# Weights in 1 MB transfers with 8192-byte rows, and the values of two attention blocks side by side

## The chip, the cores and the metric

The kernel runs on one core of a Trainium2 chip. The metric is the device time of one execution in microseconds (us): 333.23 us, the median of 3 runs (332.99 to 333.95). Its engines are PE (matrix products), DVE and ACT (element work, both also reading PE's banks), POOL (element work), and SP, which here issues nearly all transfers. All transfers run on the same 16 DMA engines.

## The reference

Three stages, all in float32 outside:

```
attention   B=4, H=8, S=768, D=64; chunks of 32 queries see 16 keys to the left, their own 32,
            8 to the right, and 8 memory keys; softmax; x = out as (3072 tokens, 512)
soft MoE    logits = x @ phi (32 slots); slot_input = softmax over tokens, transposed, @ x
            for each of 8 experts: relu(slot_input[e] @ w1[e]) @ w2[e]   (512x1024, 1024x512)
            x = softmax over slots(logits) @ slot_out
final       h = x @ w_in; solu = h * softmax(h); layer norm times g; @ w_out
```

w1 and w2 are 2 MB for each expert, 32 MB in all; w_in and w_out arrive as 64-bit floats, 4 MB each, and are turned into float32 on the chip.

## The kernel before, in words

**Attention.** The work is 32 blocks (GROUPS), each two heads by half a sequence, 12 chunks. Block g has one array kq (keys and queries, 128 rows of 3200 bytes, 400 KB, `load_qk`, L188) and two halves of values (64 rows of 3120 bytes each, 195 KB, `load_v`, L202), loaded into alternate partitions of one of four zeroed buffers vz. The loop over g issues, in this order: the score products of block g+1 (`emit_qk`, L254), the softmax steps of g+1, the load of kq g+4, weight loads (`load_e`), the value products of block g-1 (`emit_pv`, L310), the load of values g+3 (VLEAD), the transposes of g, and the spreading of kq g+3 into a zero-padded operand by POOL and ACT (`emit_spread`, L303 and L299). SP takes its transfers in that order; a load of kq waits for the products on its old contents, a load of values for `emit_pv(g-1)`.

**Weights.** They are loaded in chunks of 512 KB (128 rows of 4096 bytes) into slots of a list: eight of w_in and seven of w_out alternately, then w1 and w2 by units, then the last of w_out. A unit is half of an expert's w1 or w2, two chunks, 1 MB; there are 32 (`units`), in the order in which PE uses them. LOADS says how many chunks `load_e` issues in each block of the loop (30 in all); after the loop it issues as many as there are free slots. There are 17 slots in the areas e1, e2 and e3, the four of e3 used once only; a slot of w_out (w7); and when the attention's buffers are done, 5 in ex0 (the kq area), 6 in ex1 (the vz area) and one each in ex2 and ex3 (buffers of x). `release` puts a slot back on the list when its chunk has been used: a chunk of w_in when it has been cast, a chunk of a unit behind the products of that unit.

**Units.** After the attention, `emit_w1` (L497) and `emit_w2` (L515) run the 32 units; the transposes between them are L504. Behind each unit its two chunks are released and `load_e` is called. In between stand the casts of w_out and the softmax over slots. Then the final stage runs over 24 tiles of 128 tokens, on PE for the most part (L723).

The program states the order by hand; each engine takes its instructions in that order and waits only for what it needs.

The order of the loads stands in these lines of the loop:

```python
            if g + 4 < GROUPS:
                load_qk(g + 4)
            load_e(LOADS[g])
            if 1 <= g:
                emit_pv(g - 1)
            if g + VLEAD < GROUPS:
                load_v(g + VLEAD)
```

Of the kernel before, what the change touches and what calls it, by code (L numbers as in the profile page):

```python
# [16 lines left out]
P = 128  # L17
# [6 lines left out]
WIN = 64  # L24
REC = CH + NMEM
NREC = NCH + 1
VW = D + 1
NT = B * S
NTILE = NT // P
DM = H * D  # L30
KC = DM // P
E, SE, FF = 8, 4, 1024
NSLOT = E * SE
FC = FF // P
GT = 3
GROUPS = UNITS * 2
# [4 lines left out]
NR = GT * NSLOT  # L41
NE = 25
CAST0, CASTN, NEARLY = 3, 3.4, 8
VLEAD = 3
LOADS = [0] + [1, 1, 1, 0] + [1] * 28
LANE, SIDE = 2.6, 1

CASTU = (0, 1, 2, 3, 4, 5, 6)
# [25 lines left out]
VS = GCH * VW  # L74
# [5 lines left out]
def tile_kernel(ctx: ExitStack, tc: tile.TileContext, kr, vr, w1, w2, w_in, w_out, cst, out):  # L80
    nc = tc.nc
    pe, dve, act, pool, sp = nc.tensor, nc.vector, nc.scalar, nc.gpsimd, nc.sync
# [35 lines left out]
    def at(name, off, n, dt=FP32):  # L118
        o, size, tl = arenas[name]
        assert off + n <= size, (name, off, n, size)  # L120
        v = tl[:, o + off:o + off + n]
        return v if dt == FP32 else v.bitcast(dt)
# [3 lines left out]
    def bank(i):  # L126
        return banks[i]
# [20 lines left out]

    kq = [at("kq", nq * i, nq) for i in range(4)]
    kz = [at("kz", 2 * KS * i, 2 * KS) for i in range(2)]  # L150
    vz = [at("vz", 2 * VS * i, 2 * VS).rearrange("p (h c) -> p h c", h=2) for i in range(4)]
    sb_ = [at("s", GTOK * i, GTOK) for i in range(2)]
    atb = [at("at", GTOK * i, GTOK) for i in range(2)]
    xtb = at("xt", 0, KC * GTOK).rearrange("p (k t) -> p k t", k=KC)
# [4 lines left out]
    w_in_f = at("win", 0, KC * FF)  # L159
    w_in_sb = w_in_f.rearrange("p (k f) -> p k f", k=KC)  # L160
    mhi = at("win", 0, FF, FP32R)
    free = [at(n, 1024 * i, 1024) for n, c in (("e1", 4), ("e2", 9), ("e3", NE - 13 - FC)) for i in range(c)]
    wslot = [at(f"w{j}", 0, 1024) for j in range(FC)]
    once = free[13:]
    free.append(wslot[-1])
    whi, wlo = {}, {}

    sint = at("misc", 0, 128).rearrange("p (k s) -> p k s", k=KC)
# [18 lines left out]
    def load_qk(g):  # L187
        sp.dma_start(out=kq[g % 4], in_=kr[g])  # L188
# [8 lines left out]
            move(on, z[:, :, 0:CH], own)  # L197
            move(on, z[:, :, CH:REC], mem.to_broadcast([64, GREC, NMEM]))

    def load_v(g):  # L200
        for h in range(2):
            sp.dma_start(out=vz[g % 4][h:P:2, h, :], in_=vr[g, h])  # L202

    units = [("w1", 0, 0), ("w1", 0, 1)]
    for e in range(E - 1):
        units += [("w1", e + 1, 0), ("w2", e, 0), ("w1", e + 1, 1), ("w2", e, 1)]
    units += [("w2", E - 1, 0), ("w2", E - 1, 1)]
    chunks = [(w, j) for j in range(2 * KC) for w in ("win", "wout")][:-1]
    for u in units:
        chunks += [u[:2] + (2 * u[2] + j,) for j in range(2)]  # L210
    chunks.append(("wout", FC - 1))
    slot_of = {}
    nxt = [0]

    def more(name, n):

        free.extend(at(name, 1024 * i, 1024) for i in range(n))

    def load_e(n=99):
        while n and nxt[0] < len(chunks):  # L220
            key = chunks[nxt[0]]
            if key[0] == "wout":
                slot = wslot[key[1]]
            elif free:
                slot = free.pop(0)
            else:
                break
            slot_of[key] = slot
            if key[0] in ("w1", "w2"):
                src = (w1 if key[0] == "w1" else w2)[key[1], key[2]]  # L230
                sp.dma_start(out=slot.rearrange("p (k f) -> p k f", k=2), in_=src)
            else:
                src = (w_in if key[0] == "win" else w_out)[key[1]]
                sp.dma_start(out=slot.bitcast(I64), in_=src)
            nxt[0] += 1
            n -= 1

    def release(key):
        if slot_of[key] is wslot[-1]:
            return  # L240
        if key[0] == "win" or not any(slot_of[key] is x for x in once):
            free.append(slot_of[key])


    def kwin(i, c):
# [2 lines left out]
    def emit_qk(g):  # L248
        i = g % 4
        bk = bank(g % 2)  # L250
        for t in range(GT):
            for j in range(4):
                c = t * 4 + j
                pe.matmul(  # L254
                    out=bk[32 * j:32 * j + 32, t * 128:(t + 1) * 128],
                    lhsT=kq[i][:, KT + c * CH:KT + (c + 1) * CH],
                    rhs=kwin(g % 2, c),
                    start=True, stop=True,
                )
# [45 lines left out]
    def emit_pv(g):  # L305
        bk = bank(4 + g % 2)
        for t in range(GT):
            for j in range(4):
                c = t * 4 + j
                pe.matmul(  # L310
                    out=bk[32 * j:32 * j + 32, t * 2 * VW:(t + 1) * 2 * VW],
                    lhsT=atb[g % 2][:, c * CH:(c + 1) * CH],
                    rhs=vz[g % 4][:, :, c * VW:(c + 1) * VW],
                    start=True, stop=True,
                )

# [480 lines left out]

    with tc.manual_schedule():
        for i in range(4):
            for h in range(2):  # L800
                (pool if i < 3 else dve).memset(vz[i][:, h, :], 0.0)
            if i < 2:
                dve.memset(kz[i][0:64, KS:2 * KS], 0.0)
                dve.memset(kz[i][64:128, 0:KS], 0.0)
# [3 lines left out]
        load_qk(2)  # L808
        load_v(0)
        load_qk(3)  # L810
        load_v(1)
        load_v(2)
        emit_spread(0, "ad")
        emit_qk(0)
        emit_spread(1, "ad")
# [18 lines left out]
        for j in range(NEARLY):  # L834
# [4 lines left out]
            out=sel, in_=ident.rearrange("p (t s) -> p t s", t=4)[:, 0:GT, :], axis=AX.X, op=ALU.add  # L839
        )  # L840
        for g in range(GROUPS):
            if g + 1 < GROUPS:
                emit_qk(g + 1)
            if g == GROUPS - 2:
                area("a0", [("ex0", 5 * 1024)])
                more("ex0", 5)
            emit_softmax(g + 1)
            if g + 4 < GROUPS:
                load_qk(g + 4)
            load_e(LOADS[g])  # L850
            if 1 <= g:
                emit_pv(g - 1)
            if g + VLEAD < GROUPS:
                load_v(g + VLEAD)
            for f, hb in todo.get(g, []):
                f(hb)
            emit_t(g)
            if 3 <= g:
                emit_xt(g - 3, copy=False)
            emit_at(g)  # L860
            for f, hb in then.get(g, []):
                f(hb)
            if g + 1 < GROUPS:
                emit_exp(g + 1)
            if 3 <= g:
                emit_xtcopy(g - 3)
            for f, hb in last.get(g, []):
                f(hb)
            if 3 <= g + SPL < GROUPS:
                emit_spread(g + SPL, SPR[g % len(SPR)])  # L870
            for j, i in casts.get(g, []):
                if j not in early:
                    early[j] = win_ops(j, j)
                early[j][i]()
# [40 lines left out]
        for i in range(5, 24, 6):  # L915
            x = cb.pop(i)
# [59 lines left out]
        for x in TAIL[:first]:  # L976
# [12 lines left out]
            e3=e3,  # L989
# [7 lines left out]
def layout(inputs):  # L997
    import numpy as np

    q, k, v = inputs["q"], inputs["k"], inputs["v"]  # L1000
    mk, mv = inputs["mem_k"], inputs["mem_v"]
    f = np.float32
    a = {}
    qv = q.reshape(B, PAIRS, 2, 2, GTOK, D).transpose(0, 3, 1, 2, 5, 4)
    fill = mk[:, :, 0:1, :]
    kp = np.concatenate([np.repeat(fill, 16, 2), k, np.repeat(fill, NREC * CH - S - 16, 2)], 2)
    kp = np.stack([np.concatenate([kp[:, :, CH * i:CH * (i + GREC) - NMEM], mk], 2) for i in (0, GCH)], 1)
    kp = kp.reshape(B, 2, PAIRS, 2, KT, D).transpose(0, 1, 2, 3, 5, 4)
    a["kr"] = np.concatenate([kp, qv], -1).reshape(GROUPS, P, KT + GTOK)
    vp = np.zeros((B, H, NREC * CH, VW), f)  # L1010
    vp[:, :, 16:16 + S, 0:D] = v
    vp[:, :, 16:16 + S, D] = 1.0
    vp = vp.reshape(B, H, NREC, CH, VW)
    mp = np.ones((B, H, NCH, NMEM, VW), f)
    mp[..., 0:D] = mv[:, :, None]
    vp = np.concatenate([vp[:, :, 0:NCH], mp, vp[:, :, 1:NREC, 0:WIN - REC]], 3)
    vp = vp.reshape(B, PAIRS, 2, 2, GCH, WIN, VW).transpose(0, 3, 1, 2, 5, 4, 6)
    a["vr"] = np.ascontiguousarray(vp).reshape(GROUPS, 2, WIN, VS)
    a["w1"] = np.ascontiguousarray(
        inputs["moe_w1"].reshape(E, 2, 2, P, 2, 512).transpose(0, 4, 1, 3, 2, 5).reshape(E, 4, P, 2, 512)  # L1020
    )
    a["w2"] = np.ascontiguousarray(inputs["moe_w2"].reshape(E, 4, 2, P, DM).transpose(0, 1, 3, 2, 4))
    a["w_in"] = np.ascontiguousarray(
        inputs["moe2_w_in"].reshape(DM, FC, 4, 32).transpose(0, 2, 1, 3).reshape(KC, P, 2, 512).transpose(0, 2, 1, 3).reshape(2 * KC, P, 512)
    ).view(np.int64)
    a["w_out"] = np.ascontiguousarray(inputs["moe2_w_out"].reshape(FC, P, DM)).view(np.int64)
    c = np.zeros((P, NCONST), f)
    p = np.arange(P)
    c[p, C_ID + p] = 1.0
    c[p, C_I4 + p % 32] = 1.0  # L1030
    for r in range(4):
        c[p, C_REP + 32 * r + p % 32] = 1.0
    c[(p // 32) % 2 == 1, C_NM] = -1.0
    c[:, C_PHI:C_PHI + KC * NSLOT] = inputs["moe_phi"].reshape(KC, P, NSLOT).transpose(1, 0, 2).reshape(P, KC * NSLOT)
    c[:, C_G:C_G + FC] = inputs["moe2_g_ln"].reshape(FC, P).T
    a["cst"] = c
    return a
# [21 lines left out]
```

## Time and profile before

| | us |
|---|---|
| median of 3 runs | 333.23 |
| the profiled execution | 334.36 |
| its span | 332.5 |
| PE busy | 300.8 |
| DVE, ACT, POOL busy | 239.4, 223.1, 169.9 |

The span runs from the first instruction to the last; 1.86 us of the execution lie around it. Busy times are sums over stages with different limits, so they don't say what bounds a stage. In the profile's slices the DMA engines are busy in full from about 8 to 166 us, idle until about 190 us, and busy in part afterwards (the final stage stores and reloads a turned array and stores the result).

### The profile page before, as it was taken

What the parts mean: (1) busy time and instruction counts of PE and PEld (TensorE: products, weight loads), DVE (VectorE), ACT (ScalarE), POOL (GpSimd) and SP (SyncE); (2) the same over time, 40 slices, a digit from 0 to 9 for tenths busy, and PEclk for the clock granted to TensorE, in tenths of its full rate; (3) what the DMA queues carried; (4) which work ended last, traced back from release to release, by engine and by line L of the source; (5) the groups of instructions that cost most, each with busy time, mean ns of one, the idle gap of its engine ahead of it and who ended that gap; (6) DMA issues with size and microseconds to landing.
All of it is one profiled execution on the core that took longest, in us unless ns stands there. A gap on an engine that the chain in (4) does not pass through costs nothing.

```text
span 332.5 us, 8398 instructions
## 1 busy us (share of the span) xinstructions
PE 300.8 (90%) x3069; PEld 218.1 (66%) x3069; DVE 239.4 (72%) x432; ACT 223.1 (67%) x441; POOL 169.9 (51%) x398
## 2 busy tenths in 40 slices
PE   2979698897897789888999999999999999999996
PEld 2667576675675533332434788888888888888885
DVE  6686887797768438999117886897888778787540
ACT  3476656764765427685524779998888888888721
POOL 5436567566767023222100357777767677676600
PEclk9999999999999999999999999999999999999999
DMA  7999999999999999999950004667666756666531
GB/s 286 366 359 405 407 399 411 412 411 414 409 407 396 418 417 419 415 421 416 417 228 0 0 34 158 252 206 264 207 244 211 246 209 201 240 231 234 202 95 64
DMA packets 39433, 95.86 MB, mean 288 GB/s; under 512 B 4832, under 2 KB 15456, under 8 KB 39392
## 3 DMA queue, kind: packets, MB, share of 16 engines
q1 hardware_dynamic: 39248, 95.11, 75.3%
q8 instruction: 24, 0.39, 0.5%
q10 hardware_dynamic: 144, 0.22, 0.2%
q14 instruction: 17, 0.14, 0.1%
HBM read 78.53 MB, written 16.78 MB: 287 GB/s over the span
## 4 chain that ended last, share of the span: by engine, by line
PE 56%; DMA 32%; DVE 5%; ACT 2%; issue 2%; POOL 1%; SPq 1%; ACTq 0%; POOLq 0%
PE bank L723 37%; DMA kq_area<-in_kr_dram 19%; DMA ex_area<-in_w_dram 6%; DMA e_area<-in_w_dram 6%; PE h L635 4%; PE bank L254 3%; PE bank L310 2%; PE bank L497 1%; POOL kq_area L303 1%; PE bank L292 1%; DMA vz_area<-in_vr_dram 1%; PE bank L515 1%; PE bank L733 1%; PE t L733 1%; PE t L692 1%
## 5 line engine op out<-in xcount | busy, mean ns | idle before, releaser
L723 PE MATMUL bank<-wh_area,yh_area 128*128 128x512 f32 x552 | 129.8, 390 | 0.0
L723 PEld LDWEIGHTS bank<-wh_area,yh_area 128*128 128x128 f32 x552 | 103.4, 188 | 21.8
L303 POOL TENSOR_SCALAR kq_area<-kq_area 64x416 f32<-64x416 f32 x88 | 38.5, 443 | 38.5 <-DMA kq_area<-in_kr_dram 27.9
L254 PE MATMUL bank<-kq_area 128*32 128x128 f32 x768 | 29.8, 293 | 16.8 <-POOL kq_area L303 10.8
L706 DVE STREAM_TRANSPOSE yq_area<-yq_area 128x1024 f32<-128x1024 f32 x20 | 24.9, 1246 | 17.2 <-DMA yq_area<-z 17.2
L254 PEld LDWEIGHTS bank<-kq_area 128*32 128x32 f32 x768 | 21.0, 116 | 23.1 <-POOL kq_area L303 15.2
L650 DVE SCALAR_TENSOR_TENSOR eb_area<-h,eb_area 128x1024 f32<-128x1024 f32 x24 | 29.0, 1213 | 9.2 <-ACT eb_area L644 9.0
L295 ACT COPY s_area<-bank 128x384 f32<-128x384 f32 x32 | 15.2, 476 | 27.7 <-PE bank L292 26.1
L310 PE MATMUL bank<-vz_area,s_area 128*32 128x130 f32 x768 | 29.7, 279 | 2.2 <-ACT s_area L295 1.6
L272 DVE TENSOR_REDUCE cst_area<-bank 128x6 f32<-128x384 f32 x32 | 17.7, 554 | 19.2 <-PE bank L254 19.0
L688 POOL TENSOR_SCALAR cst_area<-cst_area 128x1 f32<-128x1 f32 x72 | 26.6, 369 | 7.6
L641 DVE TENSOR_REDUCE cst_area<-h 128x1 f32<-128x1024 f32 x24 | 29.0, 1216 | 0.9 <-PE h L635 0.9
L644 ACT ACTIVATE eb_area<-h,cst_area 128x1024 f32<-128x1024 f32 x24 | 26.6, 1110 | 1.9 <-DVE cst_area L641 1.9
L673 ACT ACTIVATE eb_area<-eb_area,cst_area 128x1024 f32<-128x1024 f32 x24 | 27.3, 1138 | 0.1
L677 POOL TENSOR_SCALAR cst_area<-cst_area 128x1 f32<-128x1 f32 x24 | 15.9, 662 | 21.7 <-ACT eb_area L644 19.8
L717 DVE TENSOR_TENSOR yh_area<-yq_area,yh_area 128x1024 fp32r<-128x1024 f32 x20 | 24.5, 1224 | 2.3 <-ACT yh_area L713 2.3
L670 ACT ACTIVATE eb_area<-eb_area,cst_area 128x1024 f32<-128x1024 f32 x20 | 23.1, 1155 | 4.3 <-DVE eb_area L650 3.8
L310 PEld LDWEIGHTS bank<-vz_area,s_area 128*32 128x32 f32 x768 | 22.3, 111 | 5.0 <-ACT s_area L295 2.8
L689 POOL TENSOR_SCALAR cst_area<-cst_area 128x1 f32<-128x1 f32 x72 | 21.9, 304 | 7.1
L713 ACT CAST yh_area<-yq_area 128x1024 fp32r<-128x1024 f32 x20 | 21.0, 1049 | 6.3 <-DVE yq_area L706 6.3
L741 ACT ACTIVATE eb_area<-bank,cst_area 128x512 f32<-128x512 f32 x23 | 15.8, 685 | 8.8 <-POOL cst_area L679 5.9
L299 ACT COPY kq_area<-kq_area 64x416 f32<-64x416 f32 (+1 forms) x34 | 12.2, 407 | 11.2 <-DMA kq_area<-in_kr_dram 11.1
(154 smaller groups left out, 534.2 us busy)
## 6 DMA issues: line engine op xcount, KB each, us to landing
e_area<-in_w_dram SPq DMA_DIRECT2D x37, 512.0 KB, 8.5
ex_area<-in_w_dram SPq DMA_DIRECT2D x26, 512.0 KB, 10.0
kq_area<-in_kr_dram SPq DMA_DIRECT2D x32, 400.0 KB, 6.3
vz_area<-in_vr_dram SPq DMA_DIRECT2D x64, 195.0 KB, 6.3
z<-eb_area SPq DMA_DIRECT2D x20, 512.0 KB, 2.7
yq_area<-z SPq DMA_DIRECT2D x80, 128.0 KB, 2.9
out_dram<-eb_area SPq DMA_DIRECT2D x23, 256.0 KB, 2.1
e_area<-in_w_in_dram SPq DMA_DIRECT2D x8, 512.0 KB, 6.4
```

Of the source, the lines that this page charges most:

```text
L254: pe.matmul(out=bk[32 * j:32 * j + 32, t * 128:(t + 1) * 128], lhsT=kq[i][:, KT + c * CH:KT + (c + 1) * CH], rhs=kwin(g % 2, c), start=Tru ...
L303: pool.tensor_scalar(out=o, in0=i, scalar1=1.0, scalar2=0.0, op0=ALU.mult, op1=ALU.add)
L310: pe.matmul(out=bk[32 * j:32 * j + 32, t * 2 * VW:(t + 1) * 2 * VW], lhsT=atb[g % 2][:, c * CH:(c + 1) * CH], rhs=vz[g % 4][:, :, c * VW:( ...
L641: dve.tensor_reduce(out=sc("nm", i), in_=fin["h"][i % 2], axis=AX.X, op=ALU.max, negate=True)
L644: act.activation(out=eb[i % FIN], in_=fin["h"][i % 2], func=ACTF.Exp, bias=sc("nm", i), accum_out=sc("s", i))
L650: dve.scalar_tensor_tensor(out=ub[i % FIN], in0=fin["h"][i % 2], scalar=-1.0 / FF, in1=eb[i % FIN], op0=ALU.mult, op1=ALU.mult, accum_out= ...
L670: act.activation(out=yb[i % FIN], in_=ub[i % FIN], func=ACTF.Identity, scale=-float(FF), bias=sc("nu", i))
L673: act.activation(out=sq, in_=ub[i % FIN], func=ACTF.Square, scale=-float(FF), bias=sc("nu", i), accum_out=sc("vs", i))
L688: pool.tensor_scalar(out=t, in0=r, scalar1=r, scalar2=xx, op0=ALU.mult, op1=ALU.mult)
L706: dve.transpose(out=yv[i % FIN].rearrange("p (f a t) -> p a f t", f=FC, a=4), in_=yq[i % FIN].rearrange("p (a f t) -> p a f t", f=FC, a=4),)
L717: dve.tensor_tensor(out=yl[i % FIN][:, sl], in0=tps(i, sl) if i < NPE else yv[i % FIN], in1=yh[i % FIN][:, sl].bitcast(FP32), op=ALU.subtract,
L723: pe.matmul(out=fin["o"][i % 2], lhsT=a[i % FIN][:, f * 128:(f + 1) * 128], rhs=w[f], start=start, stop=stop)
```

## The change

The values of two blocks, g = 2m and 2m+1, lie side by side in one of two buffers and come in two transfers of 64 rows of 6240 bytes (390 KB each); `load_v(m)` is called for even g, for the pair m = g/2 + 1. Weights of w_in, w1 and w2 come in pairs of chunks, 1 MB, 128 rows of 8192 bytes, into slots of two chunks (`free`). Single slots (`ones`) serve only the two chunks of unit 0 and the four of the last two units; w_out stays in chunks of 512 KB. A pair's slot goes back when both its chunks have been used. LOADS counts chunks as before, two in each second block. The arrays in memory are laid out for it, and the four buffers are cleared by one instruction each instead of two.

```diff
-VLEAD = 3
-LOADS = [0] + [1, 1, 1, 0] + [1] * 28
+LOADS = [0, 2, 0, 2, 0] + [0, 2] * 14
...
-    vz = [at("vz", 2 * VS * i, 2 * VS).rearrange("p (h c) -> p h c", h=2) for i in range(4)]
+    vz = [at("vz", 4 * VS * i, 4 * VS).rearrange("p (h n c) -> p h n c", h=2, n=2) for i in range(2)]
...
-    free = [at(n, 1024 * i, 1024) for n, c in (("e1", 4), ("e2", 9), ("e3", NE - 13 - FC)) for i in range(c)]
+    free = [at(n, 2048 * i, 2048) for n, c in (("e1", 2), ("e2", 4), ("e3", (NE - 13 - FC) // 2)) for i in range(c)]
...
-    once = free[13:]
-    free.append(wslot[-1])
+    once = free[6:]
+    ones = [at("e2", 8 * 1024, 1024), wslot[-1]]
...
+    for j in range(0, 2 * KC, 2):
+        chunks.append([("win", j), ("win", j + 1)])
+        chunks += [[("wout", i)] for i in (j, j + 1) if i < FC - 1]
+    for n, u in enumerate(units):
+        chunks += [[x] for x in halves(u)] if n == 0 or n >= len(units) - 2 else [halves(u)]
+    chunks.append([("wout", FC - 1)])
...
     def more(name, n):
-        free.extend(at(name, 1024 * i, 1024) for i in range(n))
+        free.extend(at(name, 2048 * i, 2048) for i in range(n // 2))
+        if n % 2:
+            ones.append(at(name, 1024 * (n - 1), 1024))
...
     def release(key):
+        slot, keys, two, kind = pair_of[key]
+        gone.add(key)
+        if not all(k in gone for k in keys) or slot is wslot[-1]:
             return
+        if kind == "win" or not any(slot is x for x in once):
+            (free if two else ones).append(slot)
...
-                    rhs=vz[g % 4][:, :, c * VW:(c + 1) * VW],
+                    rhs=vz[g // 2 % 2][:, :, g % 2, c * VW:(c + 1) * VW],
...
-            for h in range(2):
-                (pool if i < 3 else dve).memset(vz[i][:, h, :], 0.0)
+            (pool if i < 3 else dve).memset(at("vz", 2 * VS * i, 2 * VS), 0.0)
...
         load_v(0)
         load_qk(3)
-        load_v(1)
-        load_v(2)
...
-            if g + VLEAD < GROUPS:
-                load_v(g + VLEAD)
+            if g % 2 == 0 and g // 2 + 1 < GROUPS // 2:
+                load_v(g // 2 + 1)
```

## Rows read from the trace of the kernel before

**Rows 1.** Windows: stretch, us, busy by engine, TensorE clock, DMA share, GB/s.
```profile
0.00:8.00 8.00, 2.15 (x42) 2.18 (x46) 5.36 (x11) 2.72 (x5) 4.38 (x10) 1.00 0.76 282
8.00:14.00 6.00, 5.46 (x74) 3.75 (x70) 4.03 (x9) 2.44 (x6) 2.41 (x6) 1.00 1.02 402
14.00:22.00 8.00, 7.74 (x191) 6.15 (x183) 6.18 (x17) 5.89 (x15) 2.40 (x6) 1.00 0.94 317
22.00:100.00 78.00, 66.83 (x1464) 52.31 (x1459) 60.92 (x156) 50.78 (x140) 50.62 (x90) 1.00 1.03 408
100.00:106.00 6.00, 4.63 (x110) 3.87 (x102) 5.66 (x13) 2.86 (x10) 5.48 (x7) 1.00 1.02 396
106.00:124.00 18.00, 14.77 (x170) 8.18 (x167) 7.37 (x25) 6.96 (x24) 2.69 (x4) 1.00 1.02 414
124.00:166.00 42.00, 37.87 (x304) 14.09 (x301) 32.99 (x73) 28.37 (x68) 10.66 (x12) 1.00 1.03 418
```
**Rows 2.** Waits of SP: line, what ended the wait, us, times, longest.
```profile
SPq L231 <- DMA e_area<-in_w_dram: 24.3, 29, 1.0
SPq L231 <- DMA ex_area<-in_w_dram: 18.1, 21, 1.3
...
SPq L231 <- PE bank L497: 2.8, 3, 2.4
...
SPq L202 <- PE bank L310: 2.7, 1, 2.7
```
**Rows 3.** DMA issues: line, transfers, KB each, median us from issue to landing.
```profile
ex_area<-in_w_dram SPq DMA_DIRECT2D x26, 512.0 KB, 10.0
kq_area<-in_kr_dram SPq DMA_DIRECT2D x32, 400.0 KB, 6.3
vz_area<-in_vr_dram SPq DMA_DIRECT2D x64, 195.0 KB, 6.3
...
out_dram<-eb_area SPq DMA_DIRECT2D x2, 128.0 KB, 1.7
```
**Rows 4.** DMA queues: packets, MB, share of 16 engines.
```profile
q1 hardware_dynamic: 39248, 95.11, 75.3%
```
**Rows 5.** Timeline of SP near the start: start, us, line, transfers.
```profile
9.63 0.43 SPq L234 DMA_DIRECT2D e_area<-in_w_in_dram  x1
12.88 1.12 SPq L202 DMA_DIRECT2D vz_area<-in_vr_dram  x2
...
15.71 1.12 SPq L202 DMA_DIRECT2D vz_area<-in_vr_dram  x2
```
**Rows 6.** Timeline of SP from 95 to 172 us.
```profile
105.35 14.85 SPq L231 DMA_DIRECT2D ex_area<-in_w_dram  x13
123.40 13.03 SPq L231 DMA_DIRECT2D e_area<-in_w_dram  x13
```
**Rows 7.** Timeline of PE, units 0 and 1, 5, 30 and 31.
```profile
122.31 1.92 PE L497 MATMUL bank<-e_area,cst_area 128*32 128x512 f32 x16 [0.27 <-DVE cst_area L426]
...
128.81 1.07 PE L515 MATMUL bank<-e_area,hr_area 128*32 128x512 f32 x8
...
168.04 1.97 PE L515 MATMUL bank<-e_area,hr_area 128*32 128x512 f32 x8
170.24 2.21 PE L515 MATMUL bank<-e_area,hr_area 128*32 128x512 f32 x8 [0.24 <-DMA e_area<-in_w_dram]
```
**Rows 8.** Chain that ended last, around the last weights: start, us, what.
```profile
161.61 9.74 DMA e_area<-in_w_dram
...
171.40 1.05 PE bank L515 x4
```
**Rows 9.** Line 801, clearing the value buffers: ns min/median/max, first and last start.
```profile
L801 POOL MEMSET vz_area<- x6: 747/747/747, 0.7 to 4.2; 128x780 f32 x6
```
**Rows 10.** Timeline, end of the attention: spreading of kq 31, value product of block 30.
```profile
101.36 2.12 POOL L303 TENSOR_SCALAR kq_area<-kq_area 64x416 f32<-64x416 f32 x4 [0.23 <-DMA kq_area<-in_kr_dram]
...
106.52 0.87 PE L310 MATMUL bank<-vz_area,s_area 128*32 128x130 f32 x24 [0.30 <-ACT s_area L295]
```

More of the change, by code (lines that the diff above doesn't have):

```diff
@@ L198, in emit_spread, with load_v @@
             move(on, z[:, :, CH:REC], mem.to_broadcast([64, GREC, NMEM]))
-    def load_v(g):
+    def load_v(m):
         for h in range(2):
-            sp.dma_start(out=vz[g % 4][h:P:2, h, :], in_=vr[g, h])
+            sp.dma_start(out=vz[m % 2][h:P:2, h, :, :], in_=vr[m, h])
     units = [("w1", 0, 0), ("w1", 0, 1)]
@@ L207, in tile_kernel, with halves @@
     units += [("w2", E - 1, 0), ("w2", E - 1, 1)]
[L208 to L212, printed above, removed]
+    def halves(u):
+        return [u[:2] + (2 * u[2] + j,) for j in range(2)]
+    chunks = []
+    for j in range(0, 2 * KC, 2):
+        chunks.append([("win", j), ("win", j + 1)])
+        chunks += [[("wout", i)] for i in (j, j + 1) if i < FC - 1]
@@ L213, in tile_kernel @@
+    for n, u in enumerate(units):
+        chunks += [[x] for x in halves(u)] if n == 0 or n >= len(units) - 2 else [halves(u)]
+    chunks.append([("wout", FC - 1)])
+    slot_of, pair_of = {}, {}
     nxt = [0]
     def more(name, n):
-        free.extend(at(name, 1024 * i, 1024) for i in range(n))
+        free.extend(at(name, 2048 * i, 2048) for i in range(n // 2))
+        if n % 2:
+            ones.append(at(name, 1024 * (n - 1), 1024))
     def load_e(n=99):
[L220 to L225, printed above, removed]
+        while n > 0 and nxt[0] < len(chunks):
+            keys = chunks[nxt[0]]
+            kind, two = keys[0][0], len(keys) == 2
+            if kind == "wout":
+                slot = wslot[keys[0][1]]
+            elif free if two else ones:
+                slot = (free if two else ones).pop(0)
@@ L226, in load_e @@
             else:
                 break
[L228 to L231, printed above, removed]
+            for i, key in enumerate(keys):
+                slot_of[key] = slot[:, 1024 * i:1024 * i + 1024]
+                pair_of[key] = (slot, list(keys), two, kind)
+            if kind in ("w1", "w2"):
+                src = (w1 if kind == "w1" else w2)[keys[0][1], keys[0][2] // 2]
+                if not two:
+                    half = keys[0][2] % 2
+                    src = src[:, 2 * half:2 * half + 2]
+                sp.dma_start(out=slot.rearrange("p (k f) -> p k f", f=512), in_=src)
@@ L232, in load_e @@
             else:
-                src = (w_in if key[0] == "win" else w_out)[key[1]]
+                src = w_in[keys[0][1] // 2] if kind == "win" else w_out[keys[0][1]]
                 sp.dma_start(out=slot.bitcast(I64), in_=src)
             nxt[0] += 1
-            n -= 1
+            n -= len(keys)
+    gone = set()
     def release(key):
-        if slot_of[key] is wslot[-1]:
+        slot, keys, two, kind = pair_of[key]
+        gone.add(key)
+        if not all(k in gone for k in keys) or slot is wslot[-1]:
@@ L240, in release @@
             return
-        if key[0] == "win" or not any(slot_of[key] is x for x in once):
-            free.append(slot_of[key])
+        if kind == "win" or not any(slot is x for x in once):
+            (free if two else ones).append(slot)
     def kwin(i, c):
@@ L1017, in layout @@
     vp = vp.reshape(B, PAIRS, 2, 2, GCH, WIN, VW).transpose(0, 3, 1, 2, 5, 4, 6)
-    a["vr"] = np.ascontiguousarray(vp).reshape(GROUPS, 2, WIN, VS)
+    a["vr"] = np.ascontiguousarray(
+        vp.reshape(GROUPS // 2, 2, 2, WIN, VS).transpose(0, 2, 3, 1, 4)
+    )
     a["w1"] = np.ascontiguousarray(
-        inputs["moe_w1"].reshape(E, 2, 2, P, 2, 512).transpose(0, 4, 1, 3, 2, 5).reshape(E, 4, P, 2, 512)
+        inputs["moe_w1"].reshape(E, 4, P, 2, 512).transpose(0, 3, 2, 1, 4)
     )
-    a["w2"] = np.ascontiguousarray(inputs["moe_w2"].reshape(E, 4, 2, P, DM).transpose(0, 1, 3, 2, 4))
+    a["w2"] = np.ascontiguousarray(inputs["moe_w2"].reshape(E, 2, 4, P, DM).transpose(0, 1, 3, 2, 4))
     a["w_in"] = np.ascontiguousarray(
-        inputs["moe2_w_in"].reshape(DM, FC, 4, 32).transpose(0, 2, 1, 3).reshape(KC, P, 2, 512).transpose(0, 2, 1, 3).reshape(2 * KC, P, 512)
+        inputs["moe2_w_in"].reshape(DM, FC, 4, 32).transpose(0, 2, 1, 3).reshape(KC, P, 1024)
     ).view(np.int64)
```

## The prediction

> **What bounds the kernel now.** I read the windows first. From 22 to 166 us the DMA engines are busy for the whole of each stretch (share 1.02 to 1.03), and no compute engine is [rows 1]; the last weight lands at 171.4 us [rows 8], and what follows waits for no load. So the change acts up to there, and the rest follows at a fixed distance. The reader should see in rows 1 that the rate differs: 317 GB/s from 14 to 22 us, 408 in the attention, 418 where only weights are loaded.
>
> Next the queue. SP issues the loads in program order, and most of its waits there are for an earlier load [rows 2]. How many are under way follows from the time to landing: a weight transfer lands after 10.0 us, and 10.0 us x 418 GB/s = 4.2 MB = 8 transfers of 512 KB; in the attention 6.3 us x 408 = 2.6 MB, again 8 transfers (two blocks of kq, weights and two value halves, 2.67 MB) [rows 1, 3]. The bound counts transfers, not bytes. Each row is one packet: 34,432 rows by the program's shapes plus 16 for each of the 301 transfers of this queue make 39,248 [rows 4].
>
> Then the places where the queue is short. At the start SP waits 2.7 us for the first value product [rows 2], and its loads come singly [rows 5]: 8 us at 317 instead of 408 GB/s lose 0.73 MB, or 1.8 us. And at 120.2 us (105.35 + 14.85) all slots are full; the next weight goes out at 123.40, when PE has done with unit 0 [rows 6, 7]. That 3 us gap of SP is invisible in the rate (414, then 418) because eight transfers, 10 us of work, are still under way.
>
> Last the end. Units (1 MB of w1 or w2) pass PE from 122.31 us. Up to unit 29 PE finds them landed; unit 30 takes 1.97 us against the usual 1.07 (unit 5), unit 31 waits for a weight until 171.40 [rows 7, 8]. Without that wait PE would be done near 168.04 + 2 x 1.07 = 170.2 instead of 172.45: faster loads alone can win at most 2.3 us unless the units also start earlier.
>
> **The change, part by part.** The profiled execution took 334.36 us, 1.86 beyond its span; the median of the timed runs is 333.23, 1.13 lower. I work out differences on the span and add them to the median.
>
> *Start.* With rows of both blocks, SP has 1 MB more to issue before it needs a product: behind win 0 and 1 (1 MB at about 9.6 us) comes kq 6, and only then the third value pair, which waits for pv(1) instead of pv(0). Issued by then: seven kq (2.87 MB), constants (0.22), two pairs (1.60), 1.05 MB, together 5.7 MB. Before, 8 x 282 + 6 x 402 + 2 x 317 = 5.3 MB had moved by 16 us [rows 1], and the load behind pv(1) went out at 15.71 [rows 5]; so the queue just about lasts. I take all of the lost 1.8 us as won; bounds 0.5 and 2.4. The memsets clear the same cells in four instructions for eight of 0.75 us [rows 9]; the first pair's second half must wait for 2 x 1.5 us of them, where kq 0 to 2 still keep the engines busy: nothing.
>
> *Rate.* Half the packets for weights and values, 5 transfers for 8 in two blocks. No row shows a packet of 8192 bytes under full load, so I bound it. Below: rate unchanged. Above: mixed loads of 24 packets and 4 completions per engine and block ran at 408, weights alone (20.3 and 2.5 for the same bytes) at 418; taking that 2.4% as the price of those counts and extending it to the change's 16 packets gives over 4%, 426 GB/s. But the same 2.4% can come from having 2.6 MB under way instead of 4.2; then the larger transfers lift the mixed stage to 418 and the pure one not at all. I take 418 mixed and 422 pure: near the nearest row, with a small gain for the rows. From 22 us to the last kq (about 99 us) 31.4 MB took 77 us and take 75.1: 1.9 us won, bounds 0 and 3.3. Pure: 71 us, 0.7 won, bounds 0 and 1.7.
> The Trainium skill (DMA: Bandwidth & Descriptors, "Why small descriptors are slow") puts a fixed 3 cycles on each packet. By that, 4096 bytes cost 131 cycles and 8192 cost 259, an estimate of 1.1% or 422.7 GB/s pure; the trace shows no such pair of packets, and the sum would stay as it is.
>
> *Order.* Up to the last kq the old list loads 25 weight chunks, the new one 27 (29 by value pair 15): 1.05 MB, 2.5 us more ahead of the attention's last data. Values of two blocks land behind a 1 MB weight, some 4.4 us behind their even kq; pv(30) runs 5.2 us after the last kq landed (106.52 against 101.36) [rows 10], so the value pair, 1.85 MB = 4.4 us behind that kq, just arrives. Its slot wait (pv(g-1)) blocks kq g+5 and the next weights behind it on SP, but about 2.6 MB are then under way, 6 us: nothing.
> So the attention's end and unit 0 move by -1.8 - 1.9 + 2.5 = -1.2 us, to 121.1; bounds -3.2 and +2.0.
>
> *Slots.* This speaks against the change. A pair comes free only when both halves are done, odd slots serve only unit 0 and the last two. Before unit 0 is done the old lists hold 31 unit chunks, the new ones 28 (2 singles, 13 pairs), and unit 0 gives back nothing that a pair can use: unit 1 does. Up to there 13.11 + 0.22 + 12.78 + 43 x 0.524 = 48.65 MB are loaded. Rows 1 sum to 48.8 MB at 124 us, of which some 0.4 are no loads of this list: landed at 124.3 us before. Now: 124.3 - 1.8 - 1.9 - 0.2 = 120.4 us, and then the queue is dry. Unit 1 leaves PE at 122.31 + 1.92 - 1.2 = 123.0; then SP issues, and the path's latency follows: 128 KB land 1.7 us after issue on idle queues [rows 3], less 0.3 for the bytes, 1.3 to 1.4. Idle from 120.4 to 124.4: 4.0 us. Two pairs (units 1 and 2) then last 5.0 us; units 3 and 4 sit in slots that are used once, so the next comes from unit 5 (129.88 - 1.2 on PE [rows 7], data at 130.1): 0.7 more. Idle 4.7 us in all, where nothing was idle.
>
> *Sum.* Last weight: -1.8 - 1.9 - 0.7 + 4.7 = +0.3 us. PE's own work starts 1.2 earlier and would be done by 169.0, so the weight decides. The finish behind it is unchanged. 333.23 + 0.3 = 333.5 us. Because the restart hangs on unit 1, the sum is about 1.5 us plus the shift of the attention: its own range is 332.3 to 334.5.
>
> **Rivals.**
> *A, the loads win more.* If rows and depth both count (426 mixed, 428 pure), unit 0 starts 2.6 us earlier, idle is 5.0, the sum -1.8 - 3.3 - 1.7 + 5.0 = -1.8: 331.4. For it: 408 against 418. Against: both rates stand where rows are over 3 KB already, and 24 to 20 packets is a thin lever.
> The Trainium skill's rule for authors on the same page (at least 1 MiB per DMA for full bandwidth, "Rules for kernel authors") argues for A; in this trace 512 KB already run at 418 GB/s, because eight are under way.
> *B, the attention ends later.* The two extra chunks and the bunched values cost more than the start returns: start gain 0.5, rate still 408 and 418. Unit 0 comes 2.0 us later, the queue is dry from 123.8 to 127.6 and 0.5 more: -0.5 + 4.3 = +3.8; with the start gained in full +2.5, the likelier end: 335.7. It decides as soon as the attention ends more than 0.5 us later. For it: POOL already waits for kq [rows 10], and two blocks now arrive within 2 us out of 6.4.
> *C, the rows are cut at 4096 bytes*: packets stay near 39,000, rate gain only from depth: -1.8 - 1.9 + 4.5 = +0.8, or 334.0. For it: nothing; against: the rows of before are one packet each [rows 4].
> *D, the queue never runs dry* (a slot comes free earlier than I count): then the loads end some 4 us early, PE's own work decides, -1.2 - 2.2 = -3.4: 329.8. Against: the slot lists follow from the code.
>
> **Chances.** Forecast 0.40, A 0.24, B 0.22, C 0.08, D 0.06. A measurement can tell about 0.3%, 1.0 us, from nothing. Forecast and C fall mostly within that (0.36 in all), and leave a little on both sides: faster 0.32, slower 0.32. Range 331.0 to 336.0: it holds A, C and most of B, and leaves out D and B's far end.
>
> **What would show it.** Packets near 29,000 if rows are whole. Rate in 22:100 and in the weight stage: 418 and 422. Last kq landed by 100.2 us, unit 0 on PE at about 121.1. A hole of some 4 us in the DMA share right before unit 1's slot is reloaded, a shorter one 5 us later. PE's wait for the last weight until about 171.7 us. No hole, or unit 0 later than 122.8, would make it wrong.

## The result and the profile after

The changed kernel takes 338.79 us (median of 6 runs, 337.11 to 340.23), beside 333.68 us (6 runs, 332.99 to 334.63) of the kernel before: ratio 1.0146 with a 95% interval of 1.011 to 1.0181. It is slower, by about 5 us, and lies above the forecast range. The profiled execution took 338.62 us against 334.36, its span is 336.8 us against 332.5; the traces below have to explain these 4.3 us.

The windows of the kernel after, with the columns of [rows 1] and the same stretches up to 166 us:

```profile
0.00:8.00 8.00, 2.15 (x43) 2.18 (x47) 5.21 (x10) 2.72 (x5) 4.25 (x7) 1.00 0.74 287
8.00:14.00 6.00, 5.46 (x125) 3.91 (x121) 4.96 (x13) 3.65 (x10) 2.41 (x6) 1.00 0.92 308
14.00:22.00 8.00, 5.27 (x107) 4.20 (x100) 4.25 (x13) 3.57 (x9) 2.40 (x6) 0.88 1.01 409
22.00:100.00 78.00, 67.74 (x1481) 52.92 (x1480) 59.56 (x155) 50.63 (x141) 49.45 (x88) 0.99 1.02 415
100.00:106.00 6.00, 4.46 (x109) 3.52 (x108) 5.62 (x15) 3.21 (x10) 5.38 (x9) 1.00 1.01 395
106.00:124.00 18.00, 14.77 (x171) 8.84 (x174) 8.19 (x26) 6.50 (x23) 2.89 (x4) 1.00 0.93 372
124.00:166.00 42.00, 37.48 (x301) 13.48 (x289) 32.98 (x73) 28.77 (x67) 11.27 (x13) 1.00 0.96 386
```

Its queue, as [rows 4]:

```profile
q1 hardware_dynamic: 31936, 95.11, 73.0%
```

Read the last column of the windows against [rows 1], and the bytes balance. Up to 22 us the kernel after has moved 0.21 MB more: 287 against 282, then 308 against 402, then 409 against 317. Up to 100 us (415 against 408) it is 0.76 MB ahead, 1.8 us. From 106 to 124 us it loses 42 GB/s x 18 us = 0.76 MB, all of the lead. From 124 to 166 us it loses another 32 x 42 = 1.34 MB, which at 419 GB/s is 3.2 us. So the loss lies between 106 and 166 us, where the loads of the kernel before had never stopped.

Finer windows of the same kernel, the first two of 2 us, the next three of 4 to 6, the last one of 26 us that shows what the loads reach when nothing holds them:

```profile
122.00:124.00 2.00, 1.73 (x19) 0.96 (x22) 0.29 (x1) 0.24 (x1) 1.18 (x1) 1.00 0.62 262
124.00:126.00 2.00, 2.00 (x24) 0.58 (x12) 0.37 (x2) 1.84 (x4) 0.62 (x1) 1.00 0.26 70
126.00:130.00 4.00, 4.00 (x40) 1.52 (x36) 3.15 (x9) 3.30 (x8) 0.51 (x1) 1.00 0.96 297
130.00:134.00 4.00, 3.81 (x36) 0.99 (x28) 3.94 (x9) 2.91 (x6) 2.18 (x2) 1.00 0.95 365
134.00:140.00 6.00, 5.57 (x47) 2.31 (x47) 5.89 (x15) 4.34 (x12) 1.24 (x2) 1.00 0.98 396
140.00:166.00 26.00, 22.10 (x178) 8.08 (x170) 19.62 (x42) 16.38 (x39) 6.72 (x8) 1.00 1.01 425
```

There is the hole: 70 GB/s from 124 to 126 us, and a rate that is back at 425 only after 140 us. (A hole is here a stretch in which the DMA queue runs short because no slot is free.) Against 425 the five stretches from 122 to 140 us lack 0.33, 0.71, 0.51, 0.24 and 0.17 MB, together 1.96 MB or 4.6 us. From 126 to 130 us the share is 0.96 at 297 GB/s: a busy share near 1 is not the full rate when few transfers are under way.

What SP does there: first its timeline (start, us, line, transfers), then its waits from 98 to 126 us (line, what ended the wait, us, times, longest):

```profile
100.95 5.10 SPq L244 DMA_DIRECT2D e_area<-in_w_dram  x2
106.22 7.91 SPq L244 DMA_DIRECT2D ex_area<-in_w_dram  x5
124.96 9.30 SPq L244 DMA_DIRECT2D e_area<-in_w_dram  x6
```

The second and the third of the last line's six transfers, by themselves:

```profile
126.54 0.33 SPq L244 DMA_DIRECT2D e_area<-in_w_dram  x1
130.57 0.33 SPq L244 DMA_DIRECT2D e_area<-in_w_dram  x1
```

The waits:

```profile
SPq L244 <- PE bank L514: 10.8, 1, 10.8
SPq L244 <- PE bank L327: 4.9, 1, 4.9
SPq L201 <- PE bank L309: 4.7, 1, 4.7
SPq L244 <- POOL cst_area L609: 4.2, 1, 4.2
```

SP has no free slot to load from 114.13 to 124.96 us: 10.8 us in one wait, for a product of line 514 (line 497 before). Behind it one pair goes out, a second after 1.6 us, and the third only 4.0 us later. Before, the same gap was 3.2 us [rows 6], shorter than the work under way. Three shorter waits stand ahead of it, which the forecast had held to cost nothing or had not named: 4.7 us for the value buffer, 4.2 us for a cast that must finish before a pair of w_in halves is free, 4.9 us for the value product of block 31, after which its slots come free.

The first products of unit 0, those of unit 1, which end the long wait, and near the end a unit that waits for a weight, on PE (columns as [rows 7]); behind them the chain of waits (start, us, what):

```profile
122.97 0.62 PE L514 MATMUL bank<-e_area,cst_area 128*32 128x512 f32 x2 [0.27 <-DVE cst_area L443]
...
123.85 1.04 PE L514 MATMUL bank<-e_area,cst_area 128*32 128x512 f32 x8
...
167.53 1.06 PE L514 MATMUL bank<-e_area,cst_area 128*32 128x512 f32 x8 [1.30 <-DMA e_area<-in_w_dram]
```

```profile
143.87 16.31 DMA e_area<-in_w_dram
160.19 14.77 DMA e_area<-in_w_dram
175.01 1.05 PE bank L532 x4
```

Unit 0 starts at 122.97 us (122.31 before), unit 1 passes PE from 123.85 to 124.89 us, and 0.07 us later SP issues. The last weight lands at 174.96 us against 171.35 [rows 8]: 3.6 of the 4.3 us. The byte balance gives 3.2 of these; 0.7 us of the span lies behind the units and 0.4 in the balance, and neither is explained.

### The profile page after: what moved, and what is told of

The parts are those of the page before. It is cut to its first block, busy times and chain, and to the rows that moved or that the text cites. A ratio compares the mean times of both kernels' runs of the same rounds, so it can differ in the third digit from the quotient of the medians.

```text
span 336.8 us, 8277 instructions
## 1 busy us (share of the span) xinstructions
PE 300.0 (89%) x3069; PEld 217.0 (64%) x3069; DVE 237.7 (71%) x431; ACT 222.1 (66%) x441; POOL 169.2 (50%) x395
## 3 DMA queue, kind: packets, MB, share of 16 engines
q1 hardware_dynamic: 31936, 95.11, 73.0%
## 4 chain that ended last, share of the span: by engine, by line
PE 56%; DMA 24%; DVE 9%; POOL 4%; issue 2%; ACT 2%; SPq 1%; POOLq 0%; ACTq 0%; DVEq 0%
PE bank L740 36%; DMA kq_area<-in_kr_dram 13%; DMA e_area<-in_w_dram 9%; POOL kq_area L320 4%; PE h L652 4%; PE bank L271 3%; PE bank L327 3%; DMA vz_area<-in_vr_dram 2%; SPq L201 1%; PE bank L309 1%; PE bank L514 1%; PE bank L750 1%; PE t L750 1%; PE bank L397 1%; PE bank L350 1%
## 5 line engine op out<-in xcount | busy, mean ns | idle before, releaser
L271 PE MATMUL bank<-kq_area 128*32 128x128 f32 x768 | 29.1, 289 | 15.4 <-POOL kq_area L320 9.2
L327 PE MATMUL bank<-vz_area,s_area 128*32 128x130 f32 x768 | 27.9, 277 | 5.3 <-DMA vz_area<-in_vr_dram 3.5
L327 PEld LDWEIGHTS bank<-vz_area,s_area 128*32 128x32 f32 x768 | 21.2, 109 | 8.2 <-issue 3.0
L304 ACT ACTIVATE s_area<-s_area 128x384 f32<-128x384 f32 x32 | 16.9, 529 | 3.4 <-DVE s_area L295 3.4
```

The lines of the kernel that those rows point to most:

```text
L271: pe.matmul(out=bk[32 * j:32 * j + 32, t * 128:(t + 1) * 128], lhsT=kq[i][:, KT + c * CH:KT + (c + 1) * CH], rhs=kwin(g % 2, c), start=Tru ...
L327: pe.matmul(out=bk[32 * j:32 * j + 32, t * 2 * VW:(t + 1) * 2 * VW], lhsT=atb[g % 2][:, c * CH:(c + 1) * CH], rhs=vz[g // 2 % 2][:, :, g % ...
```

## Experiments

All medians are compared with the kernel before in the same session; "unit 0" is its first product on PE, "last weight" the last landing in the weight stage.

**Which half of the change costs the time.** The first kernel is that of before with the value pairs alone (its LOADS, its chunks of 512 KB); the second is the changed kernel with the values as before.

```diff
 e1: kernel before, and
+    vz = [at("vz", 4 * VS * i, 4 * VS).rearrange("p (h n c) -> p h n c", h=2, n=2) for i in range(2)]
 e2: kernel after, and
+VLEAD = 3
+    vz = [at("vz", 2 * VS * i, 2 * VS).rearrange("p (h c) -> p h c", h=2) for i in range(4)]
```

> The values of two blocks side by side, the weights as in the kernel before. Theory S (slots of two chunks run short before unit 1 is done, the DMA queue runs dry): the slots are as before, so no dry stretch, last weight at 171 us within 1, time 332.5 to 334.5. Rival V (the bunched values and the later start delay the attention, and everything hangs on its end): unit 0 at 123 us or later, time 335 to 337.

> The weights in pairs of 1 MB, the values of each block by themselves as before. Theory S: the dry stretch between 120 and 140 us stays, last weight 3 us or more later than before, time 336.5 to 339. Rival V: most of the loss is gone, time 333.5 to 335.

Values alone: 333.25 us, ratio 0.999 (0.9977 to 1.0003). Weights alone: 338.62 us, ratio 1.015 (1.0122 to 1.0177). The same stretches in both, values alone first:

```profile
124.00:140.00 16.00, 14.57 (x121) 5.19 (x123) 15.08 (x34) 11.05 (x26) 4.01 (x5) 1.00 1.03 418
140.00:166.00 26.00, 23.29 (x183) 8.36 (x175) 17.33 (x38) 15.94 (x39) 6.29 (x7) 1.00 1.03 419
```

```profile
124.00:140.00 16.00, 15.36 (x127) 5.40 (x119) 13.51 (x33) 12.40 (x28) 4.54 (x6) 1.00 0.85 311
140.00:166.00 26.00, 21.99 (x174) 8.09 (x170) 19.50 (x41) 16.38 (x39) 6.60 (x8) 1.00 1.01 426
```

Only the kernel with weight pairs has the hole (311 GB/s), and only it has the higher rate behind it (426). The whole loss belongs to the weights.

**The slots.** If the hole comes from 28 chunks in pairs instead of 31 in singles, then three more chunks close it. Two more units are loaded as singles: three of their chunks go into odd slots that otherwise wait for the last units, the fourth into the single slot that unit 0 gives back:

```diff
-        chunks += [[x] for x in halves(u)] if n == 0 or n >= len(units) - 2 else [halves(u)]
+        chunks += [[x] for x in halves(u)] if n in (0, 14, 15) or n >= len(units) - 2 else [halves(u)]
```

> The changed kernel with units 14 and 15 loaded in single chunks, which use the four odd slots that otherwise lie idle until the last two units: 31 unit chunks instead of 28 can be loaded before unit 1 is done. Theory S: the stretch from 124 to 140 us runs near 415 GB/s again, last weight 3 us earlier than in the changed kernel (about 172), time 335 to 336. Rival V, or the size of the transfers by itself: no change, 338 to 339.

333.29 us, ratio 0.9986 (0.9967 to 1.0005): this one line gives back 5.5 us, and 335 to 336 us had been expected. Its windows, SP's long wait, then its last products on PE:

```profile
124.00:140.00 16.00, 15.36 (x127) 5.50 (x123) 13.22 (x32) 12.41 (x28) 4.51 (x6) 1.00 1.01 414
140.00:166.00 26.00, 22.48 (x185) 8.41 (x178) 19.80 (x42) 16.41 (x39) 6.87 (x8) 1.00 1.01 425
```

```profile
SPq L244 <- PE bank L514: 7.7, 2, 7.2
```

```profile
168.70 1.91 PE L532 MATMUL bank<-ex_area,hr_area 128*32 128x512 f32 x12
170.38 1.05 PE L532 MATMUL bank<-e_area,hr_area 128*32 128x512 f32 x4
```

414 GB/s stand where 323 stood in the kernel after (1.96 MB less 0.33 before 124 us, by the rows above). SP's long wait is 7.2 us instead of 10.8: it has three more chunks to issue before, and goes on at 124.18 us, behind unit 0, instead of 124.96. Unit 0 still starts at 123.09 us, so the attention is as late as in the kernel after, and PE's last units follow each other without a wait for a weight: PE's own work sets the end, and faster loads could give no more here.

The count alone is tested in the kernel before, whose chunks stay single and come free one by one, by taking three of them away:

```diff
-        more("ex1", 6)
+        more("ex1", 3)
```

> The kernel before with three slots less in ex1: 28 unit chunks instead of 31 before unit 0 is done, transfers and release by chunk as before. If the count of slots by itself costs the 5 us: a dry stretch from 124 us on, last weight 3 us later, 336 to 338. If the release by pairs is the larger part: the first slot comes back at 123.4 and again with each unit, under 1 us is lost, 333.7 to 335.

336.34 us, ratio 1.0078 (1.0054 to 1.0102). A hole opens here too, with a longest wait of 7.5 us on SP (its window, that wait, units 0 and 1 on PE):

```profile
124.00:140.00 16.00, 15.37 (x123) 5.41 (x119) 13.52 (x33) 11.68 (x27) 4.07 (x5) 0.98 0.93 344
```

```profile
SPq L231 <- PE bank L497: 8.4, 2, 7.5
```

```profile
121.18 3.57 PE L497 MATMUL bank<-e_area,cst_area 128*32 128x512 f32 x16 [0.27 <-DVE cst_area L426]
```

So the count costs some 2.6 us (0.78% of 333.4), half of the loss. What is left can go with the pairs, whose longest wait is 10.8 us (unit 0 gives back nothing that a pair can use, and a pair comes free only whole), and with the later unit 0; no run takes the two apart. In this profile the first two units also ran at a lower granted clock (mean 0.93 from 106 to 124 us; their 16 products took 3.57 us against 1.92 in [rows 7]), so the price of the count is rough as well.

**The start.** In the kernel after the second value pair stands on SP behind kq 4, which waits until its buffer has been copied and used by a score product (1.2 and 1.6 us). SP's timeline, kq 3 and 4, then the pair:

```profile
3.99 3.79 SPq L187 DMA_DIRECT2D kq_area<-in_kr_dram  x2
7.89 1.12 SPq L201 DMA_DIRECT2D vz_area<-in_vr_dram  x2
```

Issued ahead of kq 4:

```diff
         load_qk(3)
+        load_v(1)
...
-            if g % 2 == 0 and g // 2 + 1 < GROUPS // 2:
+            if g and g % 2 == 0 and g // 2 + 1 < GROUPS // 2:
```

> The changed kernel with the second value pair issued before kq 4, which must wait for the first score product. Start theory: the 1.8 us that the queue loses from 8 to 16 us are won back, the attention and unit 0 come 1 to 1.5 us earlier, and since the reload hangs on unit 1, so does the end: 337.3 to 338. Rival: the attention is held by its own engines at the start and nothing moves: 338.8.

337.28 us, ratio 1.0119 (1.0079 to 1.016): 1.5 us less than the kernel after by the medians and 0.9 by the ratios, whose intervals overlap, so the times alone don't show a gain. The profile shows where it lies. The stretches at the start, at unit 0 and behind the restart, and unit 0's first products:

```profile
8.00:14.00 6.00, 5.37 (x132) 3.90 (x125) 5.04 (x13) 3.77 (x10) 2.41 (x6) 1.00 1.03 413
...
118.00:121.00 3.00, 2.40 (x16) 1.50 (x13) 1.51 (x5) 0.12 (x1) 0.05 (x1) 1.00 0.99 412
121.00:124.00 3.00, 2.90 (x16) 0.60 (x16) 0.05 (x1) 0.95 (x3) 1.76 (x1) 0.52 0.23 96
...
126.00:140.00 14.00, 13.36 (x111) 4.82 (x107) 13.00 (x31) 10.09 (x23) 4.13 (x5) 1.00 0.98 388
```

```profile
121.11 1.07 PE L514 MATMUL bank<-e_area,cst_area 128*32 128x512 f32 x2 [0.27 <-DVE cst_area L443]
```

The start is repaired (413 for 308 GB/s) and unit 0 comes 1.86 us earlier, at 121.11: the 1.8 us of the forecast's Start step were there to be won, by an edit that the change does not have. By the restart most of it was lost again in this profile, in which units 0 and 1 ran at a granted clock of 0.52 (the 1.2 GHz level): two products took 1.07 us instead of 0.62, and SP went on at 124.77 us, only 0.2 earlier than in the kernel after. The last weight still landed 1.3 us earlier (173.70), as the loads from 126 to 140 us ran at 388 GB/s and not at 359 (by the finer windows above); why is open.

**Order.** LOADS with one chunk less and the second half of the list shifted by a block, so that two chunks fewer stand ahead of the last attention data; alone, with the early second pair, and with that and the split units:

```diff
-LOADS = [0, 2, 0, 2, 0] + [0, 2] * 14
+LOADS = [0, 2, 0, 2, 0] + [0, 2] * 6 + [0, 1] + [0, 2] * 7
```

> The changed kernel with one weight pair less ahead of the attention's last values and nothing else (no second pair early, no split). The order step put 2.5 us on these two chunks. If so, unit 0 comes at 120.5 to 121.5 us instead of 123.0, unit 1 gives its slot back as much earlier, and the last weight follows: 335 to 337. If the order is worth little, the gain of the version with both came from the start: unit 0 at 122.5, 338.

> The changed kernel with the second value pair early and one weight pair less before the attention's last values, units 14 and 15 in pairs as in the changed kernel. Theory S (the slots decide): unit 0 at 120.5 us, the queue still runs dry at about 120, the reload hangs on unit 1, last weight 4 us later than with the split (172.5), time 334 to 335.5. Rival (order and start are the cause, the slots only matter with them): 331.

> Units 14 and 15 in single chunks, the second value pair issued before kq 4, and one weight pair less loaded ahead of the attention's last values (the list entry of block 18 is 1, so 25 chunks stand before the last kq as in the kernel before, not 27). Theory: unit 0 comes at 119 to 120.5 us instead of 123.1 (1.3 from the start, 2.5 from the order), PE's own work of 48.3 us behind it no longer decides, the last weight lands at 168 to 169, time 330.5 to 332. Rival (the attention's own engines hold it): unit 0 at 122 or later, 333.

| kernel | median, us | ratio (95%) | unit 0 | last weight |
|---|---|---|---|---|
| after | 338.79 | 1.0146 (1.011 to 1.0181) | 122.97 | 174.96 |
| order alone | 335.06 | 1.0034 (1.0013 to 1.0055) | 119.49 | 170.43 |
| order, early second pair | 333.32 | 1.0003 (0.9975 to 1.0031) | 119.33 | 170.12 |
| order, early pair, split units | 330.54 | 0.9914 (0.9892 to 0.9936) | 120.52 | 168.40 |

Order alone moved unit 0 by 3.5 us in its profile (that of its fastest run), further than expected, and the time by 3.7; with the early pair in both, it is 1.8 us (121.11 to 119.33). The forecast's 2.5 us lies between. Closer it can't be read: the last two rows have the same attention, and their profiles differ by 1.2 us in unit 0. The hole stays without the split:

```profile
118.00:122.00 4.00, 3.73 (x33) 1.90 (x37) 0.30 (x2) 1.72 (x4) 1.81 (x1) 1.00 0.68 283
122.00:124.00 2.00, 2.00 (x20) 0.70 (x16) 1.34 (x5) 1.69 (x6) 0.51 (x1) 1.00 0.70 221
```

That is order with the early pair: 283 and 221 GB/s, and from unit 0 to the last weight 50.79 us, against 49.04 before: 1.75 us longer, where the forecast's sum for a hole has 1.5. Its 333.32 us lie between what the two theories expected (334 to 335.5, and 331): beside it the split is worth 0.9%, 3.0 us. With the split units there is none:

```profile
106.00:124.00 18.00, 15.07 (x155) 7.86 (x147) 7.12 (x24) 7.22 (x23) 2.14 (x2) 1.00 1.01 421
124.00:140.00 16.00, 14.57 (x123) 5.45 (x123) 14.71 (x33) 10.92 (x27) 4.38 (x5) 1.00 1.02 425
```

This version beats both kernels: 330.54 us, 2.8 us under the kernel before in its session (333.38) and 8.2 under the change. Of it the values alone, with the early second pair, give this:

> Values side by side, weights in chunks of 512 KB, second value pair issued before kq 4: slots, order and row length of the weights as before. Last weight bound by the rate of 4096-byte rows (419 GB/s) but 1 to 1.5 us of the start regained: 331.8 to 332.8. If the rows of 8192 bytes are what makes the best version fast, it stays 1 us or more behind that one's 330.5.

331.69 us, ratio 0.9968 (0.9946 to 0.999). That is 1.1 us less than the kernel before by the ratio and 1.8 by the medians (333.51 in its session), out of 2.9 and 2.8: a good part of the gain comes with chunks of 512 KB as they were, from pairing the values and issuing the second pair early. It stays 1.15 us behind 330.54, so by the test set beforehand the longer rows of the weights, with the pairs that they come in, have a part in the best version too.

**What the long rows are worth.** The split kernel with transfers of 1 MB made of rows of 4096 bytes (the two halves of a slot's row lie apart in memory):

```diff
-                sp.dma_start(out=slot.rearrange("p (k f) -> p k f", f=512), in_=src)
+                    sp.dma_start(
+                        out=slot.rearrange("p (h c) -> p h c", h=2), in_=src.rearrange("h p c -> p h c")
+                    )
```

> As the version with units 14 and 15 in single chunks, transfers of 1 MB too, but each made of rows of 4096 bytes (the two chunks of a pair lie apart in memory). Theory of the rows: packets rise by 4224, the rate from 140 to 166 us falls from 425 to 418 GB/s, from 22 to 100 us from 415 to 411; time within 0.5 us of 333.3, since PE's own work ends that stage. Rival (the bytes under way give the rate): 425 and 415 stay.

333.88 us, ratio 1.001 (0.9993 to 1.0027), beside 0.9986 with long rows. Its queue and its weight stage:

```profile
q1 hardware_dynamic: 36192, 95.11, 74.5%
```

```profile
140.00:166.00 26.00, 22.48 (x185) 8.40 (x178) 20.01 (x42) 16.37 (x39) 7.07 (x8) 1.00 1.02 419
```

419 instead of 425 GB/s: in the pure stage the length of the row is all of the gain, 1.4%, and the size of the transfer none of it. Two versions whose loads end earlier show 419 and 420 in the same stretch with long rows (order alone, and with the early pair), but 427 and 426 from 140 to 158 us. In the attention (22 to 100 us) the rows make 414 against 415, nothing that one profile can tell.

The reverse, rows of 8192 bytes in transfers of 512 KB, was tried in two forms: each pair as two transfers of 64 neighbouring partitions, and of every second partition.

```diff
 neighbours:
+                for a, b in ((0, 64), (64, P)) if two else ((0, P),):
+                    sp.dma_start(out=dst[a:b], in_=src[a:b])
 every second:
+                for rows in (slice(0, P, 2), slice(1, P, 2)) if two else (slice(0, P),):
+                    sp.dma_start(out=dst[rows], in_=src[rows])
```

> As the version with units 14 and 15 in single chunks, rows of 8192 bytes too, but each pair loaded by two transfers of 64 rows, 512 KB each. Theory of the rows: 425 GB/s from 140 to 166 us and about 415 from 22 to 100 stay. Rival (the bytes under way): 418 and 410. Time 333 to 334 by both.

> Rows of 8192 bytes in transfers of 512 KB again, but a transfer takes every second partition (as the values do) instead of 64 neighbours. If the 589 ns of a packet came from 64 neighbouring partitions: 309 ns, 425 GB/s from 140 to 166 us as with 1 MB transfers, time 333 to 334; then the rows give the rate. If they came from 64-row transfers of long rows as such: near 420 us again.

Both missed the time that was expected. Neighbours: 424.53 us, ratio 1.261 (1.2559 to 1.2665). Every second: 339.11 us, ratio 1.0175 (1.0146 to 1.0204). A stretch of the first in which only weights are loaded (its last values were issued at 138.31 us, unit 0 started at 169.55; the profile is of a run of 427.33 us), and the attention and the weight stage of the second:

```profile
140.00:166.00 26.00, 15.59 (x221) 10.41 (x224) 9.88 (x31) 8.16 (x29) 4.83 (x8) 0.93 0.98 225
```

```profile
22.00:100.00 78.00, 66.01 (x1377) 52.09 (x1372) 55.42 (x147) 48.43 (x135) 46.53 (x83) 0.93 0.99 389
...
140.00:166.00 26.00, 22.20 (x179) 8.25 (x182) 23.39 (x50) 18.30 (x45) 7.95 (x9) 1.00 1.01 424
```

With every second partition the pure stage runs at 424 GB/s, so the rows give that rate at 512 KB as well. The attention, though, runs at 389 GB/s and unit 0 comes at 127.01 us. Part of that is one stop on DVE, in front of a cast, and the stretch of the loads behind it:

```profile
73.67 0.69 DVE L607 SCALAR_TENSOR_TENSOR cst_area<-e_area,cst_area 128x512 int32<-128x512 int32 x1 [7.33 <-DMA e_area<-in_w_dram]
...
74.00:78.00 4.00, 1.29 (x23) 1.18 (x24) 3.88 (x12) 1.50 (x4) 2.61 (x4) 0.59 0.53 186
```

DVE stands for 7.33 us, by the profile until a weight has landed, and the loads fall to 186 GB/s. Why it waits there, and what else slows this attention, was not tested. Fewer bytes under way don't explain it: 7.0 us from issue to landing of kq at 389 GB/s are 2.7 MB, and the kernel before ran at 408 with 2.6.

## Why the prediction was wrong

- *Direction and mechanism.* The forecast was +0.3 us for the last weight; measured are +3.6. The hole is the mechanism that it named: the slots full, the queue dry, SP waiting for unit 1, and SP's restart 2.0 us after unit 0 began, where the forecast had 1.9 (123.0 against 121.1). By 126 us the windows sum to 49.0 MB, the 48.65 MB up to the full lists and the 0.4 beside them, so the count of slots was right. That the slots cause the hole is shown by the split units, which take it away and 5.5 us with it, with unit 0 at the same time. But the loss also needs a late unit 0: order alone keeps SP's wait of 10.8 us and gives back 3.7 us. Unit 0, at 122.97 us, came later than the 122.8 that the forecast had named as a sign of being wrong.
- *Start: the step that failed.* "I take all of the lost 1.8 us as won" stood against a measured 0.5 us (0.21 MB by 22 us). The count of bytes ahead of the third value pair was sound, but an earlier place was missed: the second pair stands behind kq 4, which waits for a score product. The shortage moved from 14:22 to 8:14. Issuing that pair early shows it: 413 GB/s, and unit 0 1.86 us earlier.
- *Rate.* Near in both stages: 415 for 418 in the attention, 425 for 422 behind it. In the pure stage it is the row, since rows of 4096 bytes give 419 with 1 MB as with 512 KB. In the attention the cause stays open: values alone give 414 GB/s, weights alone 411, and two profiles of the same attention differ as much (410 and 415, the last two rows of the table). The Trainium skill (DMA: Bandwidth & Descriptors, "Why small descriptors are slow"), by which I had estimated 1.1% (its 262 cycles against 259 are 1.2%), fits: 425 against 419 are 1.4%. Packets are 31,936, not 29,000: 33 pairs save 144 each and 32 value transfers 80 each, 7,312 from 39,248, which is exact; the rows are whole and rival C is out.
- *Order.* Right in size, as far as the profiles tell: 2.5 us forecast, 1.8 and 3.5 measured. With the start at 0.5 and the rate at 1.3 us, unit 0 comes at 2.5 - 0.5 - 1.3 = +0.7; measured +0.66.
- *Slots: the second step that failed. The hole was sized in the wrong pieces.* Forecast were 4.0 us of idle time before the restart and 0.7 behind it. The rows lack 1.04 MB or 2.4 us from 122 to 126 us, and 0.92 MB or 2.2 us from 126 to 140. The first piece is smaller because three waits ahead of unit 0, which I had held to be covered by the work under way, had thinned the queue before (386 GB/s from 106 to 122 us, from the rows above: 372 x 18 less 262 x 2, by 16). What they cost by themselves no run shows; the split kernel has them too, and there PE's end waits for no weight. The second piece is the error: I let the rate be full at once after the restart, but with one or two pairs under way it is 297 GB/s from 126 to 130 us and 365 from 130 to 134, and 425 is reached only after 140. The slots are not all of that: with the same times of issue within 0.2 us, the kernel with the early second pair ran at 388 GB/s in these 14 us and lacked 1.2 us, so about 1 us of the 2.2 has a cause that stays open.
- *The balance.* The last weight is unit 0 plus a distance. Unit 0 came 1.87 us later than forecast: the start gave 1.3 less, and 415 for 418 GB/s over 78 us are 0.23 MB, 0.6 us less. The distance is 52.0 us, 2.95 more than before (49.04), where 1.5 were forecast: the second piece, 2.2 instead of 0.7 us. Together 3.3 us, the whole of the miss at the last weight (+3.6 for +0.3). The second half of this is read from the windows; no run took the slow restart away alone. The 0.7 us behind the units have no cause that I can show.
- *Rivals.* B came closest: the attention ended later by more than 0.5 us, and its far end was +3.8. Its reason was right only in part, since the rate did rise.

## What to carry to other kernels

Larger transfers make larger slots: count how many bytes can be loaded before the first slot comes back, and which product gives it back, against the time that the work under way lasts; here three chunks of 0.5 MB decided 5 us and two chunks in the order of the loads 3.7, while the longer rows were worth 1.4% of the rate. When transfers are regrouped, go through the queue in order and note for each transfer which wait stands ahead of it: a shortage that leaves one place may only move to another. And read GB/s, not the busy share, to find a thin queue.

## What the runs showed of the hardware

- While only weights were loaded (140 to 166 us), transfers to 64 neighbouring partitions ran at 225 GB/s and transfers to every second partition at 424, with rows of 8192 bytes and 512 KB in both. Why was not tested.
- The DMA share can be 0.92 at 308 GB/s and 0.96 at 297, in stretches where few transfers are under way.
- The granted clock fell to 0.52 from 121 to 124 us, after 3 us at 1.00 in which PE was busy for 2.40; the two products of unit 0 then took 1.07 us instead of 0.62. The next stretch, 124 to 126 us, shows 0.87.
